# One kernel of attention and a gated layer on one core: all its commands in a new order, part of the two-sided ones on the other engine, zero products at the start, and two biases written as constants

## The chip, the cores and the metric

The kernel runs on one core of one Trainium2 chip. The core has TensorE (PE: matmuls, with PEld for the weight loads that run beside them), VectorE (DVE), ScalarE (ACT), GpSimd (POOL) and SyncE (SP), which issues most of the transfers. The metric is the device time of one execution in microseconds, as the median of repeated runs.

## The reference, cut to what matters

```python
scores = q @ k.T / sqrt(64)  -  slope[head] * distance      # [4, 8, 768, 768]
scores = where(is_global | is_local, scores, -1e9)          # 8 first keys, or the last 96
a = softmax(scores)
x = (a @ v).transpose(0, 2, 1, 3).reshape(3072, 512)
h = x @ w_in                                                # [3072, 2048]
g = h * tanh(log1p(exp(h)))
out = g @ w_out                                             # [3072, 512]
```

With e = exp(h), tanh(log1p(e)) is 1 - 2/((1+e)^2 + 1). The kernel gets it by exp, a square of e + 1, a logarithm and an exp of the negative logarithm.

## The kernel before, in words

The 3072 tokens are cut into 12 chunks of 256 tokens. A chunk has 8 steps of attention, two heads and one block of 128 tokens in each (96 steps in all), and 8 steps of the gated layer of 256 of the 2048 hidden columns each (96 steps in all, numbered m = 8 * chunk + step). Matmuls run in f16 with numbers split into a high and a low half, so most operands are made by a copy to f16 (the high half, function `copy`) and a subtraction of it from the full number (the low half, function `rest`).

A table `acts` gives each kind of work a letter, and a string `PROGRAM` of 2109 commands such as `s26` or `Z5'` says in which order they are recorded. The recording is under a manual schedule: each engine runs its instructions in just the order in which the string brings them, SP's issues of transfers too, and waits by semaphores for what its operands need. A mark ' behind a command puts it on its other engine. A copy (`L`, `M`, `A`, `D`, `g`, `h`, `z`, `a`, `c`, `T`, and `p` in the first two chunks) is on ACT without the mark and on DVE with it. A `rest` (`E`, `Z`, `d`, and `p` later) is on POOL, or DVE with the mark. `S` is on ACT or DVE with the mark, `B` on DVE or ACT with the mark, and `J` on DVE or POOL with the mark.

These are the commands that the text needs:
- `q`, `w`, `v` issue transfers: queries and keys, a 512 KB piece of the weights, values. Piece i of the 32 weight pieces then goes through `A` (exponent), `S` (sign), `B` (bits), `C` (join), `D` (high half) and `E` (low half), and `i15`, for instance, needs pieces 28 and 30, and 30 from its thirteenth matmul on.
- `K`, `L`, `M` make the masks: `K0` and `K1` the distances, `L` the 128 columns wide ones and `M` the 232 columns wide ones of a head.
- `s` is the score matmuls of two steps (L441), `t` the largest score of each row (DVE, L455), `y` the exponentials (ACT, L464), `g` the transposes on PE with the high half (L487), `p` the low half, `W` the product with v, `R`, `T`, `U`, `V` the token rows of x with their high half, low half and turn.
- `i` is the 24 matmuls of one step of the first product (L590), `j`, `u`, `n`, `r` are the four functions on ACT (L597 exp, L601 square, L605 logarithm, L609 exp), `H` multiplies by h on DVE (L614), `J` makes sums of blocks of g (three instructions at L627 to L629) for the products that need fewer matmuls, `z` and `Z` are the halves of g, and `o` is the second product (L734, or L745 for the steps of the first chunks).
- `f` makes flags of the sizes (7 small DVE instructions from L795 on).
- `O` is a product of zeros, 128x512, into a PSUM tile that nothing reads (`keep_busy`, L403). Its operand is a tile `busy` that is filled with zeros at L146.

The bias of the square is a tile `ones`, and that of the logarithm a tile `part` (128.0 in each row).

Of the kernel before, what the change touches and what calls it, by code (L numbers as in the profile page):

```python
# [107 lines left out]
def windowed(st, tc, loc):  # L108
# [707 lines left out]
    def checks(i):  # L816
# [44 lines left out]
        D6 A8 E3 p12 W10 t17 t16 l2 i0 W13 A10' W12 y17 y14 y16 A12 C8 w16 D8 g17' s18 B10 j0 u0 D5' E5 g16' p15' R2 S10 p16 E6 g14 n0 t19 p14 t18 r0 W15 x2 y19
        V2 y18 p17 T2 H0 g19' W14 R3 s20 S7 p19 V3 B16' U2 t21 O3 X16 B7 S16 T3 A16' A7 g18 O7 w14 z0' X17 U3 t20 C7 X19 i1 i8 h102 E8 j1 S14' u1 O6 A14' C10 Z0
        D7 B14 n1 w15 l102 C16 r1 D10' H1 j8 y21 s22 C14 w9 u8 z1 n8 w18 g21' y20 r8 p21 W17 p18' X18 g20 E10' t22 W19 y22 H8 O12 E7 t23 A18' S12' D14' p20' X21
        B12' Z1 z8' o0 S9 i9 y23 i2 D16' g22 j9 E14' u9 g23' v3 n9 X20 r9 p22' W16 C12 W18 p23' o1 j2 X22 W21 u2 D12' B9' W20 n2 E16' r2 H9 R4 B18 X23 E12 A9'
        B11' Z8 i10 w22 A11 H2 T4' B13 j10 W22 U4 W23 z2 w17 w24 z9' Z9 R5 u10 i3 S11 n10 r10 j3 C11 w26 D11' A17 w20 o8 S18' u3 A13 H10 S13' z10 E11 S17' C18
        i11 n3 Z2' C9 T5 w19 V4 A15 w28 B17 D9' r3 C13 D18 D13 j11 E9' o9 H3 A22' C17 E18 B24' S15' i12 B15' u11 n11 E13' S24' D17' z3' w21 o2 A24 r11 Z10' C15
        S20 j12 E17' A20 B19' w30 D15' C24 A19' E15 u12 Z3 B20' B22' H11 n12 C20 o10 D24 w23 A28' r12 D20 S22' q6 S19 C22 i4 D22 E24' E20' B28' z11' S26 h3' o3
        H12 A26 j4 E22' i5 S21 Z11 A21' B26 u4 B21 n4 C26 r4 z12' l3 H4 C19 D19' j5 q7 C21 u5 w25 E19' D26 o11 v4 n5 r5 z4 S28' A30 Z12 A23 S23 w27 C28 i13 q11
# [4 lines left out]
        g25 j18 Q1 d9' o7 g30 a10' u18 z16' r17 W24 W29 p25' t31 Q0 y31 b10 s32 p28 n18 Z16 W26 o16 H17 X25 X28 c10 a11' r18 x4 Y1 a12 z17' p30 e0 t32 y32 t33
        d10' H18 g31' m0' y33 b12 i19 i20 g33 X30 W25 j19 Z17' z18 o17 P1' p31' u19 s34 p33' G1 W28 n19 j20 b11 W30 Y0 r19 g32 e1 u20 X31 Z18' H19 t34 m1 t35
        n20 W27 i21 X33 r20 z19' R6 T6' y35 j21 s36 u21 c11' p32' g35 t37 H20 y37 W31 p35' n21 U6 z20 v5 r21 X32 t36 V6 o18 h5 Z19 g37 i23 y36 H21 i22 R7 d11
        j23 u23 o19 q13 y34 p37' l5 X37 P2' n23 s38 G2 j22 z21 T7 U7 e2 g36 a14 Z21' m2' Z20 o20 u22 n22 P3' V7 r23 o21 r22 p36' G3' H23 X36 x5 c12 H22 t38 g34
        z23 y38 z22 t39 g38' p34' i24 W37 e3 j24 Z23 m3' u24 n24 X35 y39 W33 W32 Z22' W36 i26 P4' r24 o22 j26 o23 p38' G4 X38 g39 H24 u26 p39 X39 J24' n26 i25
        r26 H26 z24 e4 J26' W35 W38 R8 T8 m4' W39 j25 U8 u25 Z24' P5' z26' X34 W34 R9 n25 i28 r25 Q2 s40 Z26 H25 T9' j28 u28 t40 y40 V8 i27 t41 G5 g40 s42 o24
        n28 d12' J25' z25 r28 Z25' o25 j27 p40' U9 q12 u27 e5 t42 n27 V9 H28 r27 i29 y41 H27 J27 m5 i31 X40 y42 P7' g41 p41 t43 z27 j29 Z27' g42 a13 u29 p42 s44
        n29 j31 X41 t45 t44 r29 o26 y44 H29 u31 n31 y45 G7' J28 s46 J29 z28' Z28' i30 g45 z29 r31 j30 p45 g44 o27 u30 p44 e7 n30 y43 H31 X45 Z29' r30 m7' i32  # L880
# [189 lines left out]
```

## Time and profile before

| | |
|---|---|
| median of 3 runs | 591.85 us (591.48 to 592.5) |
| span of the profiled execution | 590.0 us |
| PE busy | 573.7 us (97%), 5716 instructions |
| DVE busy | 491.4 us (83%) |
| ACT busy | 488.6 us (83%) |
| POOL busy | 267.5 us (45%) |
| granted TensorE clock | 1.00 in every stretch |

The span is that of the program as the profiler sees it; the median of the runs is 1.85 us above it. A busy share is an average over the program: the engines that are busiest change on the way, which the stretches below show.

### The profile page before, as it was taken

The numbers are of one execution on the slowest core, as the hardware profiler recorded it, in microseconds if no ns is written. First come the engines' busy times: TensorE is split into PE (matmuls) and PEld (weight loads), VectorE is DVE, ScalarE is ACT, GpSimd is POOL, SyncE is SP. The second block draws the span as 40 slices with busy tenths as digits, with TensorE's granted clock in tenths as the row PEclk, the third lists the DMA queues.
The fourth block names the chain that finished last, engine by engine and source line by source line (L and its number), as shares of the span: only waits on it lengthen the run. The fifth ranks groups of instructions, "written<-read, shape, count | busy, mean of one in ns | idle before, by whom it ended". The sixth has DMA issues, their size and how long they took to land.

```text
span 590.0 us, 15156 instructions
## 1 busy us (share of the span) xinstructions
PE 573.7 (97%) x5716; PEld 474.7 (80%) x5721; DVE 491.4 (83%) x1272; ACT 488.6 (83%) x1133; POOL 267.5 (45%) x273
## 2 busy tenths in 40 slices
PE   4999999999999999999999999999999999999996
PEld 3887765676766889888889889888888988898884
DVE  5999999999998988978979789798978875863673
ACT  4999999999999899898898987778787787767670
POOL 0125424045223464576943656653652164545450
PEclk9999999999999999999999999999999999999999
DMA  8999796582574435633957463636254512241001
GB/s 246 309 319 247 153 278 182 177 173 54 160 138 102 72 73 111 148 92 71 225 98 152 93 146 72 140 81 150 48 127 73 128 31 70 54 74 55 37 1 39
DMA packets 132973, 73.78 MB, mean 125 GB/s; under 512 B 102144, under 2 KB 122624, under 8 KB 132896
## 3 DMA queue, kind: packets, MB, share of 16 engines
q1 hardware_dynamic: 132608, 72.63, 52.7%
q8 instruction: 46, 0.75, 0.6%
q14 instruction: 31, 0.25, 0.1%
q10 hardware_dynamic: 288, 0.14, 0.1%
HBM read 38.62 MB, written 6.29 MB: 76 GB/s over the span
## 4 chain that ended last, share of the span: by engine, by line


## 5 line engine op out<-in xcount | busy, mean ns | idle before, releaser
L590 PE MATMUL ph<-xT,wts 128*128 128x256 f16 x2304 | 264.8, 273 | 0.7 <-DVE gf L614 0.7
L590 PEld LDWEIGHTS <-wts 128*128 128x128 f16 x2304 | 222.8, 98 | 31.6 <-issue 2.9
L734 PEld LDWEIGHTS <-gt 128*128 128x128 f16 x1491 | 143.4, 98 | 20.1 <-issue 3.0
L157 POOL TENSOR_TENSOR gt<-gf,gt 128x896 f16<-128x896 f32 (+1 forms) x40 | 70.8, 1771 | 70.5 <-DVE gt L151 45.7
L597 ACT ACTIVATE e<-ph 128x512 f32<-128x512 f32 x96 | 56.3, 587 | 52.3 <-PE ph L590 52.0
L614 DVE SCALAR_TENSOR_TENSOR gf<-e,ph 128x512 f32<-128x512 f32 x96 | 65.4, 683 | 36.0 <-ACT e L609 27.0
L464 ACT ACTIVATE A<-A,nm 128x232 f32<-128x232 f32 (+1 forms) x192 | 88.2, 462 | 3.3 <-DVE nm L455 3.2
L157 POOL TENSOR_TENSOR hl<-A,hl 128x512 f16<-128x512 f32 (+1 forms) x42 | 51.2, 1221 | 70.6 <-ACT hl L153 48.1
L455 DVE CUSTOM_DVE_ANT_0 A<-sc,mb 128x232 f32<-128x232 f32 (+1 forms) x192 | 63.5, 375 | 12.9 <-PE sc L441 9.6
L601 ACT ACTIVATE e<-e,ones 128x512 f32<-128x512 f32 x96 | 68.7, 716 | 1.7
L605 ACT ACTIVATE e<-e,part 128x512 f32<-128x512 f32 x96 | 68.4, 714 | 1.5
L734 PE MATMUL pav<-wts,gt 128*128 128x256 f16 x402 | 66.1, 273 | 0.0
L157 DVE TENSOR_TENSOR gt<-gf,gt 128x896 f16<-128x896 f32 (+1 forms) x56 | 57.9, 1037 | 8.2 <-ACT gt L153 7.8
L609 ACT ACTIVATE e<-e 128x512 f32<-128x512 f32 x96 | 59.5, 622 | 1.4
L734 PE MATMUL po<-wts,gt 128*128 128x256 f16 x426 | 58.1, 273 | 0.0
L153 ACT ACTIVATE gt<-gf 128x896 f16<-128x896 f32 (+1 forms) x48 | 40.9, 853 | 17.4 <-POOL gf L629 7.2
L745 PEld LDWEIGHTS <-gt 128*128 128x128 f16 x306 | 29.4, 98 | 30.7 <-issue 0.4
L157 POOL TENSOR_TENSOR wts<-ws,wts 128x512 f16<-128x512 f32 x17 | 22.6, 1331 | 69.2 <-DVE wts L151 28.1
L627 POOL TENSOR_TENSOR gf<-gf 128x128 f32<-128x128 f32 x45 | 28.5, 634 | 52.4 <-DVE gf L614 45.1
L745 PE MATMUL po<-wts,gt 128*128 128x512 f16 (+1 forms) x210 | 46.7, 373 | 0.0
L151 DVE TENSOR_SCALAR gt<-gf 128x896 f16<-128x896 f32 (+1 forms) x48 | 31.3, 653 | 7.1 <-POOL gf L629 2.8
L628 POOL TENSOR_TENSOR gf<-gf 128x256 f32<-128x256 f32 x45 | 34.8, 773 | 3.5
(176 smaller groups left out, 947.2 us busy)
## 6 DMA issues: line engine op xcount, KB each, us to landing
qr<-qT SPq DMA_DIRECT2D x24, 256.0 KB, 4.6
wts<-w_in SPq DMA_DIRECT2D x12, 512.0 KB, 7.3
wts<-w_out SPq DMA_DIRECT2D x12, 512.0 KB
kr<-kd SPq DMA_DIRECT2D x32, 184.0 KB, 6.7
out<-wr SPq DMA_DIRECT2D x11, 512.0 KB, 3.2
vr<-v SPq DMA_DIRECT2D x10, 512.0 KB, 4.5
vc<-vo SPq DMA_DIRECT2D x15, 192.0 KB, 2.6
wr<-w_in SPq DMA_DIRECT2D x4, 512.0 KB, 7.9
```

The costliest lines, as they stand in the source:

```text
L153: nc.scalar.activation(out, in_, AF.Copy, scale=scale)
L157: (nc.vector if other else nc.gpsimd).tensor_tensor(out, in_, high, op=ALU.subtract)
L455: nc.vector.tensor_tensor_reduce(out=A[:, j, 0:w], in0=sc[j][:, 0:w], in1=m, scale=-1.0 / (UNIT if ci < CF32 else UNIT * SQ), scalar=3.0e3 ...
L464: nc.scalar.activation(A[:, j], A[:, j], AF.Exp, bias=nm[:, h:h + 1], scale=-1.0, accum_out=rs[:, h:h + 1])
L590: nc.tensor.matmul(ph[:, j, :].rearrange("p (b t) -> p b t", b=2), wv4[:, 2 * fb, x, c * P:(c + 1) * P], xT[:, :, y * NCC + c, :], start=( ...
L597: nc.scalar.activation(mish[m]["e"], mish[m]["h"], AF.Exp, scale=1.0 / (SV * SW), accum_out=esum[:, m:m + 1])
L601: nc.scalar.activation(e, e, AF.Square, bias=ones)
L605: nc.scalar.activation(e, e, AF.Ln, bias=part, scale=SV * SW / SG / 2.0)
L609: nc.scalar.activation(e, e, AF.Exp, scale=-1.0)
L614: nc.vector.scalar_tensor_tensor(gf, mish[m]["e"], SG / (SV * SW), mish[m]["h"], op0=ALU.subtract, op1=ALU.mult, accum_out=gsum[:, m:m + 1])
L734: nc.tensor.matmul(pos[ci][bank][:, side * HN:(side + 1) * HN], gt[:, x, i, :], w[y], start=not begun[ci][bank], stop=n == 2 and ends.get( ...
L745: nc.tensor.matmul(pos[ci][bank][:, c], gt[:, x, 2 * j + 1 - bank, :], wv4[:, 2 * fb + 1, y, c], start=not begun[ci][bank], stop=last and ...
```

## The change

The string `PROGRAM` is written anew from end to end. Of the 761 commands that may stand on either of two engines, 303 change their mark, so that there are other numbers of them on each engine: the `A` on ACT are 11 where there were 20, the `D` on ACT 21 for 15, the `z` on ACT 61 for 48, the `g` on ACT 44 for 51, the `J` on POOL 36 for 45, the `Z` on POOL 32 for 40. The zero products are 31 where there were 16, and 14 of them stand ahead of the first scores. The tile of zeros is filled first of all. The tile `part` is gone, and the biases of the square and the logarithm are constants in the instruction. All else is as it was. Line numbers of the changed kernel are two lower.

```diff
--- before.py
+++ after.py
@@ -136,14 +136,12 @@
     mt = st.enter_context(tc.tile_pool(name="mt", bufs=2))
     ps = st.enter_context(tc.tile_pool(name="ps", bufs=2, space=PSUM))
 
-    part = cp.tile([P, 1], F32, name="part")
-    nc.vector.memset(part, SV * SW / SG / 2.0)
-    ones = cp.tile([P, 1], F32, name="ones")
-    nc.vector.memset(ones, 1.0)
     busy = at.tile([P, 8, P], F16, name="AT", bufs=4)[:, 0:4, :].rearrange("p a c -> p (a c)").bitcast(BF16)
     odd = cp.tile([P, 2, 1, DM // 2], F16, name="odd")
     four = cp.tile([P, 2, 4, DM // 2], F16, name="four")
     nc.vector.memset(busy, 0.0)
+    ones = cp.tile([P, 1], F32, name="ones")
+    nc.vector.memset(ones, 1.0)
 
     def copy(out, in_, scale, other=False):
 
@@ -598,11 +596,11 @@
 
     def square_e(m):
         e = mish[m]["e"]
-        nc.scalar.activation(e, e, AF.Square, bias=ones)
+        nc.scalar.activation(e, e, AF.Square, bias=1.0)
 
     def ln_u(m):
         e = mish[m]["e"]
-        nc.scalar.activation(e, e, AF.Ln, bias=part, scale=SV * SW / SG / 2.0)
+        nc.scalar.activation(e, e, AF.Ln, bias=SV * SW / SG / 2.0, scale=SV * SW / SG / 2.0)
 
     def inverse_u(m):
         e = mish[m]["e"]
@@ -854,62 +852,63 @@
         "F": lambda i: tc.mark_branch_hint_location("general", engines=[E.PE, E.Activation, E.DVE, E.SP]),
     }
     PROGRAM = """
-        K0 L3 s0 L2' L0' K1 L1 M4 L6 w4 q1 t0 t1 y1 M3' M0' M1' L4 w2 B4 s2 S4 A4' M2 t2 g1' w0 t3 s4 O14 L5' f0 L7' y0 v0 y2 p1' y3 g2 w1 t5 p2 g0 O13 q2 q3
+        O16 w2 O17 O18 O19 q1 O20 O21 K0 L1 K1 M1 O22 O23 O24 O25 L0' w4 M3' L7' O26 O27 L6' O28 O29 L5' v0 s0 t0 L3 L2 t1 y1 M2' f0 g1' p1 s2 M0' O30 O31 w0
...
-        w31 Z5' S25 C30 x3 Z13' H6 u14 D30 C25 D25 A27 q8 s26 E30 o5 U5 n14 a8 i15 r14 z6 t27 t26 j15 u15 C27 b8 H14 E25' z14' y27 c8' Z14 o13 d8' g27' B31' p27
+        D28 E28' n13 S27 j6 A25 N0 b7 s26 D23' r13 H13 z5' S30 B30' u6 z13 i14 E23' n6 r6 q10 t27 C30 q9 Z13' B27 A27 H6 z6' U5 j14 D30 E30' Z5 o5 a8 Z6' C27
...
```

The order of the instructions shows the change at three places. The first is PE's start. Before, it begins with the scores `s0` (128 columns wide) and `s2` (232 wide), and the transposes `ph` stand behind both:

```order
L441 MATMUL sc<-kr,qr 128x128 x4
L441 MATMUL sc<-kr,qr 128x232 x4
L487 MATMUL ph<-ident,A 128x128 x2
L441 MATMUL sc<-kr,qr 128x128 x4
L403 LDWEIGHTS AT
L403 MATMUL po_202<-AT 128x512
L487 MATMUL ph<-ident,A 128x128 x6
L403 LDWEIGHTS AT
L403 MATMUL po_202<-AT 128x512
L403 LDWEIGHTS AT
```

In the changed kernel 14 zero products (the last two are shown) come first, the transposes `g1'` stand between the two scores, and two zero products behind them (in the trace each of the f32 matmuls of `s` stands as two):

```order
L401 LDWEIGHTS AT
L401 MATMUL po_130<-AT 128x512
L401 LDWEIGHTS AT
L401 MATMUL po_130<-AT 128x512
L439 MATMUL sc<-kr,qr 128x128 x4
L485 MATMUL ph<-ident,A 128x128 x2
L439 MATMUL sc<-kr,qr 128x232 x4
L401 LDWEIGHTS AT
L401 MATMUL po_130<-AT 128x512
L401 LDWEIGHTS AT
L401 MATMUL po_130<-AT 128x512
L485 MATMUL ph<-ident,A 128x128 x2
```

So `s2` moved behind a pair of transposes, and 14 products of zeros, with a load each, moved ahead of everything.

The second place is DVE's start, from the distances `K0` (the three rows from L289, or L287) to the first row of `t0` (L455, or L453). Before:

```order
L289 TENSOR_SCALAR e<-gf,n_w 128x128
L290 SCALAR_TENSOR_TENSOR e<-e,n_w 128x128
L291 SCALAR_TENSOR_TENSOR e<-e,n_w 128x128
L151 TENSOR_SCALAR mb_113<-e 128x128 x2
L295 TENSOR_SCALAR e<-e,n_w 128x232
L296 TENSOR_SCALAR e<-gf,n_w 128x8
L297 TENSOR_SCALAR e<-gf,n_w 128x8
L298 TENSOR_TENSOR e<-e 128x232
L455 ISA A,nm_158<-sc,mb_113 128x128
```

In the changed kernel:

```order
L287 TENSOR_SCALAR e<-gf,n_w 128x128
L288 SCALAR_TENSOR_TENSOR e<-e,n_w 128x128
L289 SCALAR_TENSOR_TENSOR e<-e,n_w 128x128
L293 TENSOR_SCALAR e<-e,n_w 128x232
L294 TENSOR_SCALAR e<-gf,n_w 128x8
L295 TENSOR_SCALAR e<-gf,n_w 128x8
L296 TENSOR_TENSOR e<-e 128x232
L149 TENSOR_SCALAR mb_111<-e 128x128
L149 TENSOR_SCALAR mb<-e 128x232
L149 TENSOR_SCALAR mb_111<-e 128x128 x3
L453 ISA A,nm_178<-sc,mb_111 128x128
```

Five mask tiles, one of them 232 wide, stand ahead of the first `t0` where there were two.

The third place is DVE around `U5` (a low half of x for the third chunk: the row `hl<-x,hl`; the numbers are those of the buffers). Before, the row behind `U5` is the first of `t27`, the first row shown is `Z5'`, and the low half of weight piece 30 (`E30`) stands on POOL:

```order
L157 TENSOR_TENSOR gt_1638<-gf_1593,gt_1638 128x512
L373 SCALAR_TENSOR_TENSOR ws_1632<-wc_1535,ws_1632 128x512
L157 TENSOR_TENSOR gt_1686<-gf_1636,gt_1686 128x512
L614 SCALAR_TENSOR_TENSOR gf_1709,gsum_120<-e_1634,ph_1600 128x512
L373 SCALAR_TENSOR_TENSOR ws_1688<-wc_1596,ws_1688 128x512
L561 TENSOR_TENSOR hl_1263<-x_1168,hl_1263 128x512
L455 ISA A_1783,nm1_1782<-sc_1722,mb_112 128x232
```

In the changed kernel:

```order
L612 SCALAR_TENSOR_TENSOR gf_1740,gsum_118<-e_1659,ph_1604 128x512
L149 TENSOR_SCALAR gt_1742<-gf_1740 128x512
L559 TENSOR_TENSOR hl_1633<-x_1167,hl_1633 128x512
L155 TENSOR_TENSOR wts_112<-ws_1686,wts_112 128x512
L155 TENSOR_TENSOR gt_1742<-gf_1740,gt_1742 128x512
L371 SCALAR_TENSOR_TENSOR ws_1657<-wc_1738,ws_1657 128x512
```

`E30'` (the row `wts<-ws,wts`) moved from POOL to DVE, right behind `U5`, and the low half `Z6'` (the row `gt<-gf,gt` behind it) is the next. `Z5` went the other way, from DVE to POOL.

## Rows read from the trace of the kernel before

**Rows 1.** Windows: busy time and count of each engine, granted clock, DMA share, GB/s.

```profile
0.00:15.00 15.00, 6.75 (x32) 5.09 (x33) 8.65 (x46) 7.03 (x24) 1.36 (x11) 1.00 0.88 248
15.00:60.00 45.00, 43.29 (x365) 36.14 (x369) 42.95 (x149) 43.72 (x122) 14.56 (x13) 1.00 1.03 285
60.00:120.00 60.00, 59.30 (x478) 40.91 (x477) 58.09 (x128) 58.11 (x116) 18.12 (x14) 1.00 0.75 202
120.00:185.00 65.00, 65.00 (x586) 44.34 (x585) 62.00 (x162) 63.65 (x162) 27.08 (x22) 1.00 0.60 127
185.00:400.00 215.00, 214.89 (x2361) 186.15 (x2358) 185.22 (x468) 183.91 (x433) 126.11 (x128) 1.00 0.53 111
```

**Rows 2.** The timeline of the start: start, duration, engine, line, idle before and releaser.

```profile
1.01 0.27 DVE L146 MEMSET AT<- 128x256 uint32 x1
...
6.57 0.40 DVE L298 TENSOR_TENSOR e<-e 128x232 f32<-128x232 f32 x1
...
6.86 1.22 PE L441 MATMUL sc<-kr,qr 64*128 64x128 f32 x8 [6.86 <-DMA kr<-kd]
...
8.09 0.29 DVE L455 CUSTOM_DVE_ANT_0 A<-sc,mb 128x128 f32<-128x128 f32 x1 [1.12 <-PE sc L441]
...
8.87 2.12 PE L441 MATMUL sc<-kr,qr 64*128 64x232 f32 x8 [0.78 <-DVE nm L455]
...
8.94 0.65 DVE L151 TENSOR_SCALAR mb<-e 128x232 bf16<-128x232 f32 x3
...
10.81 0.40 DVE L455 CUSTOM_DVE_ANT_0 A<-sc,mb 128x232 f32<-128x232 f32 x1 [0.55 <-PE sc L441]
...
12.54 0.17 DVE L795 TENSOR_SCALAR n_neg<-n_w 128x2 f32<-128x2 f32 x1
...
13.69 0.61 PE L403 MATMUL po<-AT 128*128 128x512 bf16 x1
...
15.30 0.29 DVE L455 CUSTOM_DVE_ANT_0 A<-sc,mb 128x128 f32<-128x128 f32 x1 [0.86 <-PE ph L487]
...
16.72 0.78 ACT L362 ACTIVATE ws<-wts 128x512 f16<-128x512 f32 x1
...
18.07 1.05 PE L441 MATMUL sc<-kr,qr 64*128 64x232 f32 x8
...
19.06 0.39 PE L403 MATMUL po<-AT 128*128 128x512 bf16 x1
```

**Rows 3.** Transfers issued: count, KB of each, median us from issue to landing.

```profile
qr<-qT SPq DMA_DIRECT2D x24, 256.0 KB, 4.6
...
wts<-w_in SPq DMA_DIRECT2D x12, 512.0 KB, 7.3
...
kr<-kd SPq DMA_DIRECT2D x15, 132.0 KB, 4.5
```

**Rows 4.** The timeline further on, around `o5`, `U5` and `i15`.

```profile
116.02 0.68 DVE L157 TENSOR_TENSOR gt<-gf,gt 128x512 f16<-128x512 f32 x1
...
117.00 2.76 PE L745 MATMUL po<-wts,gt 128*128 128x512 f16 x12
...
119.03 0.68 DVE L561 TENSOR_TENSOR hl<-x,hl 128x512 f16<-128x512 f32 x1
...
119.44 1.30 POOL L157 TENSOR_TENSOR wts<-ws,wts 128x512 f16<-128x512 f32 x1 [7.00 <-ACT wts L153]
...
119.60 1.58 PE L590 MATMUL ph<-xT,wts 128*128 128x256 f16 x13
```

**Rows 5.** Groups of ACT by line: count, busy us, mean ns, idle before.

```profile
L601 ACT ACTIVATE e<-e,ones 128x512 f32<-128x512 f32 x96 | 68.7, 716 | 1.7
L605 ACT ACTIVATE e<-e,part 128x512 f32<-128x512 f32 x96 | 68.4, 714 | 1.5
L609 ACT ACTIVATE e<-e 128x512 f32<-128x512 f32 x96 | 59.5, 622 | 1.4
```

**Rows 6.** Groups of DVE by form: a copy of a weight piece.

```profile
L151 DVE TENSOR_SCALAR wc<-wts 128x512 f32<-128x512 f32 x10 | 5.3, 529 | 0.0
```

More of the change, by code (lines that the diff above doesn't have):

```diff
@@ L861, in windowed @@
[L861 to L868, printed above, removed]
@@ L873, in windowed @@
[L873 to L880, printed above, removed]
@@ new lines, in windowed @@
+        B18 j3 o8 o9 B11 A11' C11 H10 u3 E9' S18' i11 S17' A18' B17' D11 E11' z10 Z10' B13' S13' A17' n3 r3 C18 z2 Z2' C17 B15' o10 w19 A19 H3 D18 E18 i12
+        D17' A15' o2 v3 h3 j11 u11 l3 E17' S15 C15 n11 z3 Z3' w20 r11 H11 w24 z11' B22 D15 j12 u12 S24 w28 C13 E15 n12 A20' q6 B19 A22' D13 E13' i4 o3 q7 S19
+        S22' C22 Z11' o11 A24 B24' C24 r12 q11 S20 A26' B20 D24' j4 D22 u4 n4 C20 D20 E20 w21 C19 E24' H12 r4 H4 E22' c7 d7' D19 E19' w23 S23' A21 B21 z12
+        S21' S26 C21 B26' i5 j5 u5 v4 n5 V4 Z12' r5 S28' C26 D26 B28 A28' i13 j13 u13 B23 z4 D21 H5 o12 w30 A30' C28 E26 i6 a7 w27 T5' E21' Z4' A23 C23 o4 w25
@@ new lines, in windowed @@
+        D28 E28' n13 S27 j6 A25 N0 b7 s26 D23' r13 H13 z5' S30 B30' u6 z13 i14 E23' n6 r6 q10 t27 C30 q9 Z13' B27 A27 H6 z6' U5 j14 D30 E30' Z5 o5 a8 Z6' C27
+        u14 n14 b8 w29 i15 o13 c8' B25' S25' C25 r14 H14 z14' Z14' y27 g27 j15 p27 w31 D27' E27 u15 n15 r15 D25 t26 y26 d8' g26 H15 z15' i7 j7 B31' u7 s24 t24
+        A31' t29 p26' V5 h4 i16 X27 Z15' q8 y24 g24 S31' A29' E25 o6 X26 p24 j16 t28 n7 y28 C31 t25 r7 g28' l4 y29 B29' g29' p28' x3 H7 S29 D31' X24 E31 x4
+        C29 u16 s30 z7 Z7 o14 t30 n16 r16 H16 c10 d10' y25 p29' X29 D29 i17 i18 a9' t31 z16' Z16' j17 g25' c9' d9' E29 u17 y30 j18 o15 g30' u18 n17 Q1 r17 o7
@@ new lines, in windowed @@
+        Q0 a11 n18 r18 H17 z17 p30 W27 p25 P0 W29 Y1 X28 o16 b9 s32 a10 W28 y31 X30 G0 e0' g31 t33 i19 j19 W26 H18 z18' m0 p31' X31 y33 i20 W24 t32 y32 u19
+        g32 a12' n19 r19 Z17' P1' b10 G1 g33 b12 H19 s34 t35 j20 o17 p33 u20 n20 p32 r20 Y0 t34 e1 m1 X25 y35 g35 W30 i21 j21 u21 n21 Z18' X32 r21 H20 v5 W25
+        R6 W31 p35 s36 z20 Z20 T6' i22 U6 z19 Z19 c11 t37 o18 o19 R7 h5 H21 j22 t36 l5 y37 V6 X33 X35 P2' G2 g37 T7 y36 g36 i23 p37' z21 U7 e2 m2' u22 n22
+        Z21' p36' r22 P3' G3' b11 j23 s38 t38 y34 V7 c12 H22 t39 g34 p34' u23 n23 r23 H23 o20 o21 z22 Z22' e3 d11' m3' P4' y39 X36 g39' i24 W36 q12 j24 z23
@@ new lines, in windowed @@
+        Z23' u24 n24 r24 H24 W33 W32 y38 i26 J24 X37 X34 o22 j26 g38 p38' W37 p39 X39 z24 G4 X38 u26 n26 Z24' e4 m4 r26 H26 J26' i25 j25 u25 n25 W39 R8 T8 U8
+        W35 o23 P5 r25 W34 z26 Z26 W38 R9 T9 H25 V8 Q2 J25' U9 i28 j28 u28 s40 t41 i27 t40 y40 G5 z25' g40' s42 Z25' p40 n28 r28 o24 o25 t43 j27 H28 u27 e5
+        n27 r27 s28 t42 X40 H27 J27 y42 g42 p42' V9 X42 m5' y41 g41 P7' x5 i29 Y2 j29 u29 z27 p41' X41 n29 r29 d12 s44 t45 y45 i31 j31 t44 Z27' G7' u31 n31
+        r31 o26 H29 J28 J29' z28 y44 e7' Z28' H31 g45 p45' g44 s46 i30 o27 m7' X45 j30 u30 P6' G6' z29 Z29' q13 n30 t46 y43 p44' r30 y46 H30 i32 j32 u32 t47
@@ new lines, in windowed @@
+        y47 a14 J30 n32 o28 o29 b14 W41 g47' z30 Z30' X44 r32 H32 i33 e6 m6' W45 J31' a13 J32 z31 Z31' p47 X47 v6 j33 i34 u33 n33 r33 g46 p46 z32 j34 g43'
+        p43' W42 X43 H33 J33' u34 W40 W44 R10 n34 r34 c13 Z32' X46 d13 H34 h6 T10' U10 o30 i35 j35 u35 n35 o31 W47 l6 W46 b13 W43 c14 V10 R11 I3' i36 Q3 s50
+        t50 z33 t51 o32 d14' J34' z34 Z34' s48 y50 Z33 o33 q15 y51 g50 T11' p50 X50 t49 r35 y49 g49 p49 j36 u36 H35 n36 x6 i38 r36 t53 y53 g53 U11 V11 j38 u38
+        J35' t48 H36 Y3 n38 r38 i37 J36' y48 z36 p53' X53 t52 z35' Z35' g51' p51' a16 H38 v7 g48 s54 c16 t55 y55 j37 o34 o35 u37 i39 p48' X48 n37 r37 J38'
@@ new lines, in windowed @@
+        Z36' q14 z38' X49 t54 H37 y52 J37 i40 y54 g54' b16 o36 W49 h7 Z38 z37' Z37 j39 p54' W53 o37 g52 p52' X52 u39 n39 r39 H39 J39' l7 c15 j40 u40 n40 W48
+        r40 H40 J40 a15 i43 d15' X54 z40 W52 R12 b15 z39' Z39' g55' j43 u43 n43 r43 i41 T12' j41 u41 n41 r41 q16 Z40 s56 t56 X51 t57 p55' H41 J41' s52 H43 o38
+        o39 I4 c17 y56 g56 y57 J43' z41 i42 j42 u42 n42 X55 W54 W55 W50 z43 W51 r42 Q4 g57' U12 p57' X57 Z41' V12 R13 H42 i45 s58 t58 j45 u45 p56' J42' t59
+        n45 r45 Z43' y58 g58 T13 U13 o40 d16 z42 y59 i44 j44 p58' s60 t61 u44 V13 t60 n44 H45 X56 a17' q17 x7 y61 g61 p61 o41 Z42' r44 H44 J44 y60 i46 c18'
@@ new lines, in windowed @@
+        u53 n53 r53 H53 y65 g65' u52 n52 r52 s66 t67 b19 p65 y64 H52 i54 t66 y66 Y5 X70 g64 i56 j54 X65 J52 h9' l9 z52 u54 W70 W65 X71 j56 W68 J53 a20 b20 n54
+        r54 W69 Z52' g66' p66 p64' H54 z53 u56 Z53 x9 n56 o51 J54 y67 r56 H56 J56 c20' X64 z54 Z54 o52 i55 g67' j55 u55 W64 i58 n55 r55 j58 z56 H55 u58 o53
+        n58 r58 o54 p67 Z56' R16 T16 W71 X66 W66 i57 J55' z55 H58 J58 j57 u57 n57 d20 U16 X67 W67 R17 r57 d19' i59 Z55' j59 H57 u59 n59 s72 q20 t72 t77 y77
+        g77 p77 t73 J57' t76 z58 Z58' y73 r59 H59 o55 I6' Q6 i62 j62 u62 J59' y72 s74 V16 T17 i60 X77 g73' p73' X73 F0 z57 Z57' n62 o56 U17 z59' Z59 y76 q23
@@ new lines, in windowed @@
+        r68 H68 z67 i69 t83 h11 p81 y82 i71 j71 g82 p82 d22' a22' b22 u71 s84 n71 r71 Z67' X81 X82 T19' U19 o65 J68' y83 t84 y84 l11 x11 t85 y85 V19 H71 j69
+        u69 g84' o66 p84 g85' z68 i70 Z68' s86 X84 o67 o68 n69 r69 j70 u70 n70 Y7 H69 J69 i72 z69 p85' J71' z71' Z71' r70 H70 q22 a23 b23 t87 t86 y86 Z69' J70
+        i73 z70' Z70' j72 u72 W84 n72 o69 c23' r72 W82 j73 u73 n73 X85 H72 d23 y87 J72 g83 p83' W80 X83 i76 g87' z72' W85 o70 g86' p86 Z72' r73 H73 p87 W81
+        j76 u76 n76 r76 H76 J73' R20 T20' X86 i74 j74 o71 z73' Z73' X87 I8' Q8 W86 u74 n74 r74 d24 i75 j75 H74 J74 z74 J76' U20 u75 W83 W87 R21 Z74 i77 j77
@@ new lines, in windowed @@
+        r85 R22 J84 W94 i86 z84' Z84' j86 H85 X95 T22' U22 W95 o82 i87 j87 o83 o84 u87 R23 T23' U23 u86 n86 r86 J85' n87 r87 Y9 z85' Z85 H86 s76 J86 z86 V22
+        V23 i89 H87 J87' Z86' z87 Z87 j89 u89 n89 o85 r89 i88 j88 u88 H89 J89 z89' n88 Z89 r88 H88 J88' o86 i90 j90 u90 i91 z88 Z88 n90 r90 H90 j91 o87 I10'
+        Q10 Y10 i93 u91 n91 r91 H91 j93 u93 J90' z90 Z90' o88 k0 i92 o89 o90 n93 r93 H93 J91 z91 J93 z93' j92 u92 i94 n92 r92 Z91' H92 J92 z92 o91 Z92 j94 u94
+        n94 i95 Z93 r94 H94 j95 u95 J94' k1 k3 z94' n95 r95 H95 o92 Z94' o93 z95 k2 Z95' o94 o95 I11' k5 Q11 k4
```

58 lines of the change are left out of this document (20 added, 38 removed).

## The prediction, on record before the result

> **What bounds the kernel now.** I read the stretches first [rows 1]. PE is busy 43.29 of 45 us from 15 to 60, 59.30 of 60 to 120, and without a gap from there: 65.00 of 65, then 214.89 of 215. But up to 185 us DVE is nearly as full, 42.95 of 45, 58.09 of 60, 62.00 of 65, and ACT is too, 43.72, 58.11 and 63.65. Behind 185 us DVE has 30 us to spare in 215 (185.22) and PE alone sets the pace. So time can come from two places: the start, where PE does 6.75 us in 15, and waits of PE ahead of 185 us, 1.71 + 0.70 us in all. The matmuls themselves are the same before and after, but for one zero product more in the stream (below). Whatever PE is earlier at 185 us it keeps to the end; nothing behind it can add a gain, only eat one.
>
> The timeline of the start then shows what the first 15 us are made of [rows 2]. The first queries and keys land at 6.86. The scores `s0` take 1.22 us, and DVE, done with the distances at 6.97 (6.57 + 0.40), waits 1.12 us for them. It waits again 0.55 us for `s2` at 10.81, and 0.86 us at 15.30 for transposes: 2.53 us in three places. PE is slow meanwhile: eight score matmuls of one shape take 2.12 us at 8.87 and 1.05 at 18.07, and one zero product 0.61 at 13.69 and 0.39 at 19.06. That is a factor of two, as between the two levels of 1.2 and 2.4 GHz, although the granted clock stands at 1.00 in every stretch [rows 1]; I go by the durations.
>
> Where DVE feeds PE later on shows in the fourth view [rows 4]: `Z5'` ends at 116.70 (116.02 + 0.68) and `o5`, which reads it, begins at 117.00. PE was busy with scores until then, so 0.30 us is all that PE could have been ahead there.
>
> **The change, part by part.** *Constants as biases.* The square and the logarithm take 716 and 714 ns with a tile as bias, and the exponential of the same form, which has none, 622 ns [rows 5]. If they come down to that, ACT has (94 + 92) ns x 96 = 17.9 us less to do, 24 of the 96 steps (4.5 us) by 185 us, where it counts. Bounds: nothing, if the two functions are simply slower, or 17.9. I take 17.9. Alone it gives little: DVE, as full as ACT, isn't relieved, and behind 185 us PE covers it all. Filling the tile `part` was hidden under the wait for the first data; taking it out gives nothing.
>
> *The marks.* I counted what stands on DVE up to `U5`, which ends at 119.71 [rows 4], command by command with the mean of each form: 112.3 us before, 112.2 after. It gets eight exponent copies more (8 x 0.53 = 4.2 us [rows 6]) and loses six high halves of weights, four of exponentials and some smaller ones. ACT has 112.4 us ahead of `j15` before and 110.0 after, most of it the biases. So DVE has no less work ahead of the place that matters, and what it can gain is its idle time at the start. Behind `U5` stands `E30'`, 0.68 us like any such row [rows 4], which gives 119.71 + 0.68 = 120.39 less what DVE saves. Before, `E30` was on POOL and ended at 120.74 (119.44 + 1.30), just when `i15`, begun at 119.60, came to its thirteenth matmul, 12 x 0.109 us (13 take 1.58, the last 0.27) later, at 120.9 [rows 4]. So after, PE can be ahead there by 0.5 us plus what DVE saves. I take off 0.3 us for the time from the end of such a row to the first matmul on it (as `Z5'` and `o5`). `Z5` itself goes to POOL, 1.30 us a row, which has 40 us free in 60 [rows 1]; cost nothing if it starts at once, 1.30 - 0.68 = 0.6 us if `o5` waits for it.
>
> *Zero products.* 14 stand ahead of `s0`. Their operand is filled at 1.01 + 0.27 = 1.28 us at the latest [rows 2], and PE has nothing else until 6.86. At full speed a 512-column product follows the next by (2.76 - 0.39) / 11 = 0.215 us [rows 2, 4], at half by 0.43: the block ends between 1.3 + 3.0 = 4.3 and 1.3 + 6.0 = 7.3. At the late end it costs 0.4 us, at the early end nothing. One more product in the rest of the stream costs 0.215, on a PE that waits there anyway. Its use is the clock: if PE is at full level when the data land, `s0` takes 1.22 x 1.05 / 2.12 = 0.6 us, ends at 7.5, and the wait of 1.12 us is gone; DVE meanwhile does three more masks (0.65 us for three of 232 columns [rows 2]) ahead of `t0` and is ready at 7.6.
>
> *The order behind it.* `s2` now stands behind the transposes `g1'`, which wait for `y1`: DVE's `t0` and `t1` take until 8.6, the exponentials to 9.6, the transposes some 0.3. So `s2`'s first half ends at 10.4 at full level, 10.9 at half. DVE fills that time with mask tiles and the flags `f` (seven small instructions, 0.17 us the first [rows 2], so some 1.2) and comes to `t2` at 10.3: 8.6 + 2 x 0.22 + 1.2. Of the 0.55 us wait I count 0.3 as saved, and of the 0.86 us, whose place in the new order isn't the same, 0.6. The sum is 1.1 + 0.3 + 0.6 = 2.0 us. Bounds: 0.75, if the clock is at half level again from `s2` on (1.1 kept in part), and 3.5, if these and the small waits to 60 us all go.
>
> The Trainium skill has a rule on this, in "TensorE: Matmul & The Clock Gate", section "Part 1: The HAM clock gate": throttled is the default, activity releases it, and idling brings the throttle back. By it the zero block lifts the clock before the data come, but the sparse piece behind `s0`, where PE waits for `y1`, may lose it again; the first would give the 2.0 us above, the second some 0.75. The two speeds of the start agree with two levels [rows 2]; which work decides between them they don't show.
>
> *Transfers.* SP issues `w2` `q1` `w4` for `w4` `q1` `w2`. Ahead of `w4`'s end lie two sets of queries and keys (256 + 2 x 132 KB each) and two weight pieces of 512 KB [rows 3], 2064 KB; at 248 GB/s [rows 1] 8.3 us, so it lands at 9.2 at the earliest if the first bytes leave 0.9 us into the span, 12.2 with half of such a piece's 7.3 us on top. Counting DVE's rows from 7.6 on, `A4'` wants it at 13.4. It costs nothing, with some 1 to 4 us to spare; `w2`, third before, was first read at 16.72 [rows 2], which is the latest it can have landed.
>
> **The sum.** DVE saves 2.0; at `i15` PE may be ahead by 0.5 + 2.0 - 0.3 = 2.2; `o5` was 0.3 from the limit, so part of that was there already: I take 2.0. 590.0 - 2.0 = 588.0 us of span. The median is 1.85 us above the span before, 591.85, and I keep that distance: **589.9 us**.
>
> **Rivals.** 0.2% (1.2 us) is about what a measurement of this kernel can tell from no change.
>
> *Eaten gain* (0.25): the clock falls back behind `s0`, or POOL's `Z5` (0.6 us late) or another piece holds PE at the first chunks, which leaves 0.75 of the 2.0, or nothing. For it: PE was already without gaps from 120 on, and DVE's sum is unchanged. Against: 2.53 us of plain waits. It gives 591.0 (590.7 to 591.9).
>
> *More* (0.13): all waits of DVE to 60 us go (3.5), and ACT's 4.5 us less by 185 lets the 0.7 us of PE's gaps from 60 to 120 close too: 3.5 + 0.7 = 4.2, which gives 587.6.
>
> *Slower* (0.18): `w4`, third in the queue, comes late. `A4'` stands in DVE's row, and `t6` and all behind it wait. It decides from 13.4 + 2.0 = 15.4 on, where the gain is used up; at 16.72, the latest that the third place allows, it costs 16.7 - 15.4 = 1.3, so 593.2. For it: the queue is at 0.88 of its engines' time in this stretch [rows 1]. Against: the bytes.
>
> The forecast itself (1.2 to 3 us off, 588.8 to 590.7) has 0.44. Faster by over 0.2%: 0.44 + 0.13, and no more: 0.57. Within: 0.25, slower: 0.18. The range reaches from the greater gain to the late piece, 587.4 to 592.9, which leaves out a tenth on either side.
>
> **What would show it.** The score matmuls `s0` at about half their time, DVE's first wait gone, the sum of DVE's waits to 60 us smaller by 2; the two biased functions at 622 ns; `i15`'s start 2 us earlier than 119.60, and PE still without gaps from 185 on. Wrong if: the zero block runs past 6.86 at half level, `w4` lands behind 13.4, or PE has new waits behind 60 us; or if PE's speed itself is not the same, since the sum takes each matmul's time for given.

## The result

The changed kernel takes 596.94 us (median of 4 runs, 595.67 to 597.38), the kernel before 591.66 (4 runs): a ratio of 1.0086, 95% interval 1.0069 to 1.0103. It is slower by 5.3 us, where 2.0 us less was forecast. The profiled execution has a span of 595.5 us.

These are the stretches of the changed kernel, in the columns of [rows 1]:

```profile
0.00:15.00 15.00, 12.29 (x50) 5.57 (x51) 8.70 (x49) 6.89 (x24) 1.37 (x11) 0.89 0.88 235
15.00:60.00 45.00, 43.13 (x361) 36.15 (x364) 43.34 (x144) 43.24 (x121) 13.47 (x12) 1.00 1.01 256
60.00:120.00 60.00, 60.00 (x490) 42.02 (x491) 58.76 (x134) 58.20 (x120) 15.99 (x13) 1.00 0.95 244
120.00:185.00 65.00, 64.63 (x581) 43.95 (x580) 59.71 (x157) 60.87 (x157) 26.15 (x22) 1.00 0.46 101
185.00:400.00 215.00, 210.54 (x2295) 180.69 (x2294) 185.20 (x473) 181.64 (x430) 100.16 (x101) 1.00 0.52 110
```

Up to 120 us PE loses nothing by the new order: it has no gap between 60 and 120, where it had 0.70 us. From 120 to 185 there is one of 0.37 us (64.63 busy of 65), where there was none, and most of the loss stands in the last row. PE is busy 210.54 of 215 us where it was busy 214.89, a gap of 4.46 us in a stretch in which there was one of 0.11. DVE is as busy as before there (185.20), ACT a little less (181.64 for 183.91): neither is full. So work isn't too much; it comes too late.

The start of the changed kernel shows that, in this execution, even the gain was not where it was forecast. The timeline, as in [rows 2]:

```profile
1.28 6.14 PE L401 MATMUL po<-AT 128*128 128x512 bf16 x14 [1.28 <-DVE ones L144]
7.35 0.72 PE L439 MATMUL sc<-kr,qr 64*128 64x128 f32 x8
8.10 0.29 DVE L453 CUSTOM_DVE_ANT_0 A<-sc,mb 128x128 f32<-128x128 f32 x1 [0.69 <-PE sc L439]
11.31 1.04 PE L401 MATMUL po<-AT 128*128 128x512 bf16 x2
11.40 0.40 DVE L453 CUSTOM_DVE_ANT_0 A<-sc,mb 128x232 f32<-128x232 f32 x1 [0.64 <-PE sc L439]
14.65 0.29 DVE L453 CUSTOM_DVE_ANT_0 A<-sc,mb 128x128 f32<-128x128 f32 x1 [0.98 <-PE sc L439]
15.57 0.42 DVE L149 TENSOR_SCALAR wc<-wts 128x512 f32<-128x512 f32 x1
```

The 14 zero products end at 7.42, and `s0` begins at 7.35 and not at 6.86. It takes 0.72 us instead of 1.22, which gives the delay back and no more: `t0` begins at 8.10 where it began at 8.09. At 11.31 two zero products take 1.04 us, which is 0.43 for the step to the next and 0.61 for the last, both at half level (at full level it would be 0.215 + 0.39 = 0.60). The granted clock is back at half (1.2 GHz) in the two microseconds from 12:

```profile
12.00:14.00 2.00, 2.00 (x9) 0.97 (x9) 1.67 (x10) 2.00 (x10) 0.00 (x0) 0.50 1.07 295
```

Between the block and there PE had waited 1.42 us for the first exponentials. In the timeline above, DVE's three waits are 0.69, 0.64 and 0.98 us, 2.31 in all, where 2.53 stood before [rows 2] and 0.5 were forecast. The copy `A4'` at 15.57 shows no wait: its piece was there.

PE came ahead nevertheless, for one part by the 0.70 us of gaps that went between 60 and 120 us. The rows that answer to [rows 4]:

```profile
117.30 0.69 DVE L559 TENSOR_TENSOR hl<-x,hl 128x512 f16<-128x512 f32 x1
117.90 0.68 DVE L155 TENSOR_TENSOR wts<-ws,wts 128x512 f16<-128x512 f32 x1
118.50 1.69 PE L588 MATMUL ph<-xT,wts 128*128 128x256 f16 x14
```

`i15` begins at 118.50, 1.10 us ahead of 119.60, with `E30'` done just then (118.58). So far the sign was right and the size about half. A lead read off two profiles is good to a microsecond at best, though: in four profiles that begin with the order of before (that kernel, biases alone, the new rest, four buffers with the order of before), `i15` begins between 119.29 and 121.31.

### The profile page after: what moved, and what is told of

It reads as the page before. It is cut to its first block, busy times and chain, and to the rows that moved or that the text cites. A ratio compares the mean times of both kernels' runs of the same rounds, so it can differ in the third digit from the quotient of the medians.

```text
span 595.5 us, 15177 instructions
## 1 busy us (share of the span) xinstructions
PE 580.7 (98%) x5733; PEld 475.3 (80%) x5736; DVE 492.4 (83%) x1302; ACT 482.2 (81%) x1132; POOL 245.6 (41%) x243
## 4 chain that ended last, share of the span: by engine, by line
## 5 line engine op out<-in xcount | busy, mean ns | idle before, releaser
L155 POOL TENSOR_TENSOR hl<-A,hl 128x512 f16<-128x512 f32 (+1 forms) x44 | 54.5, 1243 | 104.1 <-ACT hl L151 41.4
L612 DVE SCALAR_TENSOR_TENSOR gf<-e,ph 128x512 f32<-128x512 f32 x96 | 65.5, 684 | 37.5 <-ACT e L607 30.6
L155 POOL TENSOR_TENSOR gt<-gf,gt 128x896 f16<-128x896 f32 (+1 forms) x32 | 56.6, 1772 | 58.3 <-ACT gt L151 30.2
L155 DVE TENSOR_TENSOR gt<-gf,gt 128x896 f16<-128x896 f32 (+1 forms) x64 | 67.1, 1049 | 7.6 <-ACT gt L151 7.2
L453 DVE CUSTOM_DVE_ANT_0 A<-sc,mb 128x232 f32<-128x232 f32 (+1 forms) x192 | 63.6, 375 | 10.7 <-PE sc L439 8.1
L151 ACT ACTIVATE gt<-gf 128x896 f16<-128x896 f32 (+1 forms) x61 | 52.1, 856 | 19.3 <-DVE gf L627 12.2
L607 ACT ACTIVATE e<-e 128x512 f32<-128x512 f32 x96 | 60.1, 626 | 2.2
L599 ACT ACTIVATE e<-e 128x512 f32<-128x512 f32 x96 | 60.0, 626 | 2.2
L603 ACT ACTIVATE e<-e 128x512 f32<-128x512 f32 x96 | 60.0, 625 | 2.0
L625 POOL TENSOR_TENSOR gf<-gf 128x128 f32<-128x128 f32 x36 | 20.1, 559 | 48.7 <-DVE gf L612 48.7
L462 ACT ACTIVATION_READ_ACCUMULATOR A<-A,nm 128x1 f32 x192 | 36.0, 187 | 0.0
L527 PEld LDWEIGHTS <-AT 104*128 104x128 f16 (+1 forms) x888 | 32.8, 97 | 3.7 <-DMA AT<-hl 1.1
```

The costliest lines, as they stand in the source:

```text
L151: nc.scalar.activation(out, in_, AF.Copy, scale=scale)
L155: (nc.vector if other else nc.gpsimd).tensor_tensor(out, in_, high, op=ALU.subtract)
L453: nc.vector.tensor_tensor_reduce(out=A[:, j, 0:w], in0=sc[j][:, 0:w], in1=m, scale=-1.0 / (UNIT if ci < CF32 else UNIT * SQ), scalar=3.0e3 ...
L462: nc.scalar.activation(A[:, j], A[:, j], AF.Exp, bias=nm[:, h:h + 1], scale=-1.0, accum_out=rs[:, h:h + 1])
L599: nc.scalar.activation(e, e, AF.Square, bias=1.0)
L603: nc.scalar.activation(e, e, AF.Ln, bias=SV * SW / SG / 2.0, scale=SV * SW / SG / 2.0)
```

## What PE waits for behind 180 us

The waits of PE from 180 us to the end (what waited, for what, us in total, times, longest) list nothing for the kernel before, and this for the changed one:

```profile
PE ph L588 <- DVE gf L612: 2.0, 4, 0.9
PE sc L439 <- DVE ws L194: 1.3, 1, 1.3
PE pav L732 <- DVE gt L155: 0.6, 1, 0.6
PE sc L527 <- DMA AT<-hl: 0.6, 1, 0.6
```

That is 4.5 us in 7 waits. The rest of the 6.6 us between 1.1 ahead and 5.5 behind isn't in a row of waits; a matmul's row is 0.27 us long where the next can follow in 0.11, so each wait hides up to 0.16 us in a row that counts as busy, about 1 us for the seven, and shorter waits hide altogether.

The first line says how: `i` of one step fills a PSUM tile `ph`, there are two of these, and the tile is free when `H` (L612) of the step two before has read it. `H` comes last in the chain `j`, `u`, `n`, `r` on ACT. ACT's waits from 185 to 330 us, first of the kernel before:

```profile
ACT e L597 <- PE ph L590: 7.2, 8, 1.9
ACT gt L153 <- POOL gf L629: 3.1, 2, 2.5
ACT hl L153 <- DVE xmax L540: 2.4, 2, 1.4
...
ACT hl L153 <- DMA AT<-hl: 0.6, 2, 0.4
...
```

and of the changed kernel:

```profile
ACT hl L151 <- DMA AT<-hl: 6.2, 4, 2.0
ACT e L595 <- PE ph L588: 3.7, 4, 1.6
ACT A L462 <- DVE nm L453: 2.3, 4, 1.3
ACT gt L151 <- POOL gf L627: 2.3, 2, 1.7
...
ACT hl L151 <- DVE xmax L538: 0.6, 2, 0.4
```

Before, the largest line of ACT's idle time is `e<-ph`: it is ready for the next step and waits for PE, which costs nothing. Now the largest line is `hl<-A` behind a transfer. `g` copies the exponentials to the high half in a tile `hl`, of which there are three; a tile is free when the transposing transfer (`X`, or `V` for x) that reads it has landed. From 185 to 330 us four of ACT's copies in the new order come while that transfer is still on its way, where two came before, and they wait 6.2 us for 0.6. One of the four waits, on ACT, PE and SP's queue:

```profile
208.59 1.23 SPq L504 DMA_TRANSPOSE AT<-hl  x1
...
213.67 0.63 ACT L151 ACTIVATE hl<-A 128x512 f16<-128x512 f32 x1 [1.87 <-DMA AT<-hl]
214.21 0.58 ACT L595 ACTIVATE e<-ph 128x512 f32<-128x512 f32 x1
...
218.01 0.69 DVE L612 SCALAR_TENSOR_TENSOR gf<-e,ph 128x512 f32<-128x512 f32 x1
218.82 0.39 PE L588 MATMUL ph<-xT,wts 128*128 128x256 f16 x2
```

`X40` begins to be issued at 208.59, and the copy `g41`, which takes over its tile, starts only at 213.67, 5.1 us later. (The other three copies, at 190.49, 260.03 and 274.84, start 3.7 to 5.0 us behind the issue of theirs, at 186.83, 255.34 and 269.81.) The exp `j29` stands behind `g41`, though `i29` ended at some 212.5; `H29` ends at 218.70, and `i30` starts at 218.82, as soon as its `ph` is free. From here on ACT is almost without a pause until 228, and the delay is handed on from step to step until it meets a place where PE has nothing left over: 0.90 us at 235.48. This reading is theory 4 of the experiments; it says why the chain is late, which theory 1 only states (the new order behind 180 us frees `ph` too late). The others were that the quicker functions upset the timing (2), that the loss is made at the start (3), and that the marks make it.

## The experiments

Medians are given with that of the kernel before in the same session (592.03, 592.00 and 591.79 us in the three sessions).

**Biases alone.** The order of before, constants as biases.

```diff
-        nc.scalar.activation(e, e, AF.Square, bias=ones)
+        nc.scalar.activation(e, e, AF.Square, bias=1.0)
-        nc.scalar.activation(e, e, AF.Ln, bias=part, scale=SV * SW / SG / 2.0)
+        nc.scalar.activation(e, e, AF.Ln, bias=SV * SW / SG / 2.0, scale=SV * SW / SG / 2.0)
```

> The kernel before with only the two biases written as constants; its order is kept. Theory 1 (the new order behind 180 us brings the freeing of the PSUM tile of h too late, whatever the biases): PE is the bound there already, so within 0.7 us of the kernel before. Theory 2 (quicker functions on ACT upset the timing and cost the time): 594 or more, with waits of PE behind 185 us that the kernel before does not have.

Measured: 591.42 us, ratio 0.9995 (0.9982 to 1.0009). No difference that the measurement shows. Theory 2 falls.

**The new order with tiles as biases.** The two lines above the other way round, in the changed kernel, with the tile `part` back.

> The changed kernel with the biases as tiles again; the new order and the zero products are kept. Theory 1: the late chains get 4 x 0.09 us longer each, so it is slower still, 598 to 606. Theory 2: it loses the cause of the loss and comes back to 590 to 592.

Measured: 599.22 us, 1.0137 (1.0111 to 1.0164). The constants are worth some 2.3 us (599.22 - 596.94; 3.0 by the ratios of the two sessions) in the new order, where ACT is late, and nothing that shows in the old one.

**New start, old rest.** The string up to `o21` as in the changed kernel, then all that is left in the order and with the marks of before.

```diff
-        ... H23 o20 o21 z22 Z22' e3 d11' m3' P4' ...
+        ... H23 o20 o21 s28 d11 q13 X37 a14 X36 x5 z23 y38 ...
```

> The new order up to the command o21 (some 180 us), and from there the remaining commands in the order and with the marks of before; biases as constants. Theory 1: the gain of some 1.1 us at 180 us stays and the waits behind are gone, so 590.0 to 591.2. Theory 3 (the loss is made at the start, and the waits behind 185 us only pay for PE being ahead): 594 to 597.

Measured: 595.15 us, 1.0053 (1.0027 to 1.0080). By its number this looks like theory 3, but the cut made a wait of its own. At the seam the transfers `X37` and `X36` stand behind the issue of `q13`, `X36` begins to be issued only at 183.80, and PE waits for it:

```profile
184.19 0.25 PE L527 MATMUL sc<-vo,AT 128*128 128x64 f16 x3
186.99 0.26 PE L527 MATMUL sc<-vc,AT 104*128 104x64 f16 x3 [2.55 <-DMA AT<-hl]
```

Behind that PE has no wait in a row until the end. This wait and the lower clock behind it cost some 4.05 us (2.55 + 1.5, last section); 595.15 less that is 591.1, in the range of theory 1. But that is an estimate, so another cut follows below.

**Old start, new rest.** The order of before up to `i21`, then all that is left as in the changed kernel.

```diff
-        ... i21 X33 z19' R6 T6' y35 j21 ...
+        ... i21 j21 u21 n21 X32 r21 H20 ...
```

> The order and marks of before up to the command i21 (some 157 us) and from there the remaining commands in the new order and with the new marks; biases as constants. Theory 1: the waits from 180 us on come back, some 7 us less what PE has as a lag more, so 595 to 599. Theory 3: about 591.5, as before.

Measured: 597.47 us, 1.0093 (1.0068 to 1.0118). The whole loss is there without the new start. PE's waits behind 180 us are again 1.6 us for `gf`, 1.3 for `ws`, 1.5 for a transfer (in the profiled execution, the longest of the four with 600.76 us). Theory 3 falls.

**Four buffers for `hl`.** The changed kernel with one more tile; `A` is cut to the columns that it uses, to make room.

```diff
-        A = at.tile([P, 2, W], F32, name="A", bufs=3)
+        A = at.tile([P, 2, WIDE], F32, name="A", bufs=3)
-        pend[t] = (pend[t], at.tile([P, 2, 2, W], F16, name="hl", bufs=3))
+        pend[t] = (pend[t], at.tile([P, 2, 2, W], F16, name="hl", bufs=4))
```

> The changed kernel with four buffers for hl instead of three (and the tile A cut from 256 to its 232 used columns to make room). Theory 4 (the copies hl<-A, which waited 6.2 us for transfers between 185 and 330 us on ACT, put ACT's later work behind, and that holds PE): these waits go, PE's waits behind 180 us fall from some 7 us to 3 or less, 592 to 594. If the waits are only one symptom of an order that is tight everywhere: within 1 us of the changed kernel, 596 to 598.

Measured: 590.61 us, 0.9969 (0.9954 to 0.9985). All of the loss is gone, and 1.4 us more, which theory 4 hadn't expected (592 to 594): this version beats both kernels. ACT's waits from 185 to 330 us have no line for a transfer any more:

```profile
ACT e L595 <- PE ph L588: 6.8, 6, 2.8
ACT gt L151 <- POOL gf L627: 2.3, 2, 1.8
...
ACT hl L151 <- DVE xmax L538: 0.4, 2, 0.3
```

ACT waits for PE again, 6.8 us, as before the change. PE has no line of waits behind 180 us, and in the long stretch it is as full as ever:

```profile
185.00:400.00 215.00, 214.90 (x2354) 185.52 (x2352) 191.50 (x486) 186.59 (x439) 104.48 (x105) 1.00 0.57 114
```

So theory 1 needs theory 4 as its cause: with a tile free in time, the same order holds.

**New start, old rest, another cut.** Ahead of `i21`, where the two orders have done nearly the same commands.

> As the first try of a new start with the old rest, but cut earlier, ahead of i21 (some 157 us), where the two orders have done nearly the same commands, so that no transfer of the seam is late. Theory 1 (new start some 1.1 us ahead, loss behind it): 590.0 to 591.5. Theory 3 (the start's lead is lost whatever comes behind): 594 to 597.

Measured: 592.54 us, 1.0017 (1.0003 to 1.0030). It is 1 us over what theory 1 expected, and 1.5 us under the 594 to 597 of theory 3. The seam still costs PE waits, 0.5 us for a transposing transfer and 0.4 for `gf` between 150 and 170 us, so what the new start gives can't be read from it to a microsecond. Its ten times reach from 590.56, which is the profiled one, to 594.76.

**Old marks in the new order.** Each two-sided command on its engine of before.

```diff
-        ... j29 u29 z27 p41' X41 n29 r29 ...
+        ... j29 u29 z27 p41 X41 n29 r29 ...
```

> The changed kernel's order of all commands, but with the marks of before: each two-sided command is on the engine on which it was before. If the marks (more on DVE, less on POOL) make the loss: 590 to 593. If the order makes it: 596 or more, since order and marks were made for each other and the marks of before fit the new order worse.

Measured: 682.03 us, 1.1547 (1.1500 to 1.1593). Order and marks only work together, and going back to the old marks cures nothing; whether the new marks had a share in the loss can't be read from a version that is so much slower. PE then waits 12.7 us for `gf` and 11.1 for transposing transfers behind 180 us, and the granted clock is 0.97 from 185 to 400 us.

**Zero products alone.** Fourteen of them ahead of the order of before, and the tile of zeros filled first.

```diff
+        O16 O17 O18 O19 O20 O21 O22 O23 O24 O25 O26 O27 O28 O29
         K0 L3 s0 L2' L0' K1 L1 M4 L6 w4 q1 t0 t1 y1 ...
```

> The kernel before with 14 zero products ahead of s0 and the tile of zeros filled first; order, marks and biases of before. If the block lifts the clock for the scores and that carries to the end: 0.5 to 1.2 us faster, 590.5 to 591.2. If DVE and ACT set the pace until 185 us and the block only runs in idle time, or delays s0 by the 0.5 us that it ran over in the changed kernel: 591.5 to 592.3.

Measured: 592.72 us, 1.0017 (1.0002 to 1.0033), a little slower, and 0.4 us over the second of the two ranges. In its profile (an execution of 594.69 us) the block ends at 6.07, ahead of the data, `s0` takes 0.71 us, and the first wait of DVE falls to 0.59; yet PE waits 2.3 us for `gf` between 60 and 120 us, where there was 0.7. An early lead isn't a gain by itself in the order of before.

**Four buffers with the order of before** (and constants as biases, `A` cut as above).

> The kernel before, its order and marks, with the constants as biases, four buffers for hl and the tile A cut to 232 columns. Theory 4 (three buffers are too few for the new order only): ACT waits 0.6 us for such a buffer between 185 and 330 us here and PE never, so the fourth gives nothing, 591 to 592.3. If the fourth buffer is a gain by itself, whatever the order: 590.5 or less, as with the new order.

Measured: 591.61 us, 0.9999 (0.9990 to 1.0008). No difference that the measurement shows: the order of before doesn't need the fourth tile.

**The cut of `A` alone**, in the changed kernel.

> The changed kernel with the tile A cut to 232 columns alone, hl still in three buffers. If the fourth buffer made the gain of e5: 596 to 598, as the changed kernel. If the narrower A made it: 590 to 592.

Measured: 596.72 us, 1.0074 (1.0055 to 1.0093), as the changed kernel; ACT's line for transfers is there with 5.6 us. So it is the fourth tile.

**Four buffers without the zero block.** The version that won, less the 14 products ahead of `s0`.

> e5 (new order, four buffers) without the 14 zero products ahead of s0. If the block's lead at the start is kept to the end: 0.5 to 1.5 us slower than e5, 591.1 to 592.1. If it gives nothing that lasts: 590.0 to 591.0.

Measured: 593.05 us, 1.0021 (1.0012 to 1.0030), some 3 us slower than with the block (1.0021 against 0.9969). Both expectations were too small. Without it `s0` takes 1.23 us, `t2` begins at 12.44 and `i15` at 119.67; with it (four buffers) `s0` takes 0.71, `t2` begins at 10.97 and `i15` at 118.44. That is 1.2 us of the 3; the rest wasn't followed.

**Four copies later.** The changed kernel with three buffers; only these places of its string are changed:

```diff
-        g41 P7' x5 i29 Y2 j29 u29
+        P7' x5 i29 Y2 j29 u29 g41
-        j26 g38 p38' W37 p39 X39 z24 G4 X38 u26
+        j26 W37 p39 X39 z24 G4 u26 g38 p38' X38
-        g53 U11 V11 j38 u38
+        U11 V11 j38 u38 g53
-        g52 p52' X52 u39 n39 r39
+        u39 n39 r39 g52 p52' X52
```

> The changed kernel, three buffers, with only four of the waiting copies moved: g38, g41, g52 and g53 stand behind the exp and the square (g52 behind the whole chain) of the step that they stood ahead of. Theory 4 (it is what stands behind the waiting copy on ACT that costs): PE's waits behind 180 us fall by half or more, 592.5 to 595. If the wait only moves along with the copies: 596 to 598.

Measured: 593.96 us, 1.0035 (1.0021 to 1.0050). Moving four copies takes back (1.0086 - 1.0035) x 592 = 3.0 of the 5.3 us, within what theory 4 expected. ACT's line for transfers is gone from 185 to 330 us, and PE's waits behind 180 us are

```profile
PE ph L588 <- DVE gf L612: 1.2, 3, 0.4
PE sc L527 <- DMA AT<-hl: 0.5, 1, 0.5
PE sc L439 <- DVE ws L194: 0.2, 1, 0.2
```

1.9 us for 4.5. What is left stands behind no wait of ACT for a transfer in that stretch; it wasn't followed further.

## Why the prediction was wrong, step by step

**What failed.** The step that failed is "Behind 185 us DVE has 30 us to spare in 215 (185.22) and PE alone sets the pace", with "whatever PE is earlier at 185 us it keeps to the end", which was drawn from it. It took a share of busy time for slack at every place. The 30 us were there, and are there after the change (185.20 busy of 215), but they lay in the right places only in the order of before: ACT's idle time stood in front of `j`, where it waits for PE. The new order puts 6.2 us of idle time in front of the copies, behind tiles `hl`, and the chain that frees `ph` comes late: PE, without a wait there before, waits 4.5 us in rows, and with a fourth tile not at all. The prediction counted what stands on each engine ahead of a milestone up to 185 us and looked at no order behind that. Buffers weren't looked at anywhere: how soon a command takes over a tile that a transfer still reads is in the order, with the number of tiles, and could have been counted.

**The start.** The term "DVE saves 2.0" was mis-sized for this execution. DVE's three waits lost 0.22 us (2.53 to 2.31). The block ended at 7.42, past even the late end of its bounds (7.3), and the clock was at half level again by 11.3, which was the rival *eaten gain*. "TensorE: Matmul & The Clock Gate" of the Trainium skill, section "Part 1: The HAM clock gate", has it that activity releases the throttle and idling brings it back; the trace agrees, with 0.72 us for `s0` behind the block and a granted clock of 0.50 from 12 us on, behind the sparse piece.

But the same commands don't always go this way. In the seven other profiles that start with this order the block ends between 5.84 and 6.93, ahead of the data (6.90 to 7.22), and in two of them the clock doesn't fall behind it. One of these is the new start with the old rest, in its second cut (the row of 12.00:14.00 has the columns of [rows 1]):

```profile
7.90 0.29 DVE L453 CUSTOM_DVE_ANT_0 A<-sc,mb 128x128 f32<-128x128 f32 x1 [0.50 <-PE sc L439]
9.29 0.62 PE L485 MATMUL ph<-ident,A 128*128 128x128 f32 x2 [1.40 <-ACT A L462]
10.84 0.60 PE L401 MATMUL po<-AT 128*128 128x512 bf16 x2
10.93 0.40 DVE L453 CUSTOM_DVE_ANT_0 A<-sc,mb 128x232 f32<-128x232 f32 x1 [0.37 <-PE sc L439]
...
12.00:14.00 2.00, 1.87 (x14) 1.30 (x13) 1.94 (x13) 2.00 (x9) 0.00 (x0) 1.00 1.08 290
...
117.08 2.78 PE L588 MATMUL ph<-xT,wts 128*128 128x256 f16 x24
```

PE waits as long for the exponentials (1.40 us for 1.42), yet the granted clock stays at 1.00. DVE waits 0.50 and 0.37 us, the third wait is gone, 1.7 us less than before in all, and `i15` begins 2.5 us ahead of 119.60. (In the other, with tiles as biases, the waits are 1.8 us less and `i15` is 1.4 us ahead.) Where the clock falls, DVE's three waits sum to 1.8 to 2.3 us, and `i15` is 0.8 to 1.4 us ahead in the five such profiles with the new marks. So 2.0 us is about what this start gives if the clock holds, and how often it does can't be told from eight profiles, nor what decides it.

The limit at `i15` was another one, too. The sum let it hang on `E30'`. This ended at 118.58, within 0.2 us of the forecast (120.39 - 2.0): DVE was done with `U5` 1.7 us earlier (117.99 for 119.71), though its waits at the start gave only 0.2; the rest came in places that the sum doesn't have. But PE, without a gap from 60 on, had its own work until 118.50, so a faster DVE gave `i15` nothing more. The lead of 1.10 us is more than the 0.70 us of gaps that went, and it hangs on the block: without it, with four buffers, `i15` begins at 119.67.

**The biases.** Right in size and place. The square and the logarithm now take as long as the exponential behind them (626 ns):

```profile
L599 ACT ACTIVATE e<-e 128x512 f32<-128x512 f32 x96 | 60.0, 626 | 2.2
L603 ACT ACTIVATE e<-e 128x512 f32<-128x512 f32 x96 | 60.0, 625 | 2.0
```

716 and 714 ns became 626 and 625. The Trainium skill gives some 93 ns for such an operand ("ScalarE: Activation LUTs", section "What ACT_TABLE_LOAD costs"); the rows give 90. "Alone it gives little" held: 0.9995.

**`E30'` and `Z5`.** The two places were right: `E30'` ended as `i15` began, and PE had no gap there, so none for `Z5` on POOL.

**The transfers.** `w4` wasn't late; `A4'` came at 15.57 without a wait, some 2 us behind the time that was counted for it, since DVE's waits hadn't gone. The late end of the piece's landing has a slip: half of 7.3 us on top of 9.2 is 12.9 and not 12.2, which leaves 0.5 us to spare, not 1. The rival *slower* had the right sign by luck: a late transfer it was, but one that frees a tile, 170 us further on. No rival had it, though the sign "PE has new waits behind 60 us" was named.

## What to carry to other kernels

That PE has no gap and the others have over 10% to spare doesn't say that an order can be exchanged: ask in front of which instruction each engine's idle time stands. Idle time in front of work that waits for the bound engine is slack; the same time in front of a copy whose tile isn't free is a delay for all that stands behind it. When commands are put in a new order, count for each pool of buffers how soon a tile is taken again behind the transfer that reads it; where that is tighter, one more tile or a copy a few places later may give back more than all the rest of the order gives.
